# A three-stage attention and FFN kernel: five weight conversions, two attentions, two weight sums and twelve y stores are put elsewhere

## Chip, cores, metric

One core of one Trainium2 chip. The metric is the device time of one execution in microseconds (us); lower is better.

## What is computed

The inputs are `x` (8 batches, 8 heads, 512 positions, 64 wide) and `state` (8, 8, 32, 64), and five weights that arrive as 64-bit floats. Per batch and head, x reads the state and the state reads x:

```python
a = softmax(scale * x @ state.T);   xread = a @ state      # 512 rows
a2 = softmax(scale * state @ x.T);  sread = a2 @ x         # 32 rows
X = concat([xread, sread], axis=2)                          # 544 rows per batch, heads side by side: 512 wide
h = relu(X @ moe_w_in);             Y = (h * h) @ moe_w_out # 512 -> 2048 -> 512
out = (((Y @ w1) * (Y @ w2)) @ w3) @ w_out2                 # 512 -> 1024 -> 1024 -> 512
```

## The kernel before, in words

Matmuls run on pairs of halves: a 32-bit float is written as a high and a low part (`split`, L81 to L83: a cast on ScalarE, a subtraction on VectorE), and a product takes three passes. Since xread is `a @ state`, the kernel forms `state @ w_in` per batch once (`make_sw`, L480) and multiplies it with the turned softmax `aT` (`h_tile`, L515).

**First stage.** A list `order` holds the tiles (c, f): batch c of the 512-row reads, f one of the 16 blocks of 128 of the 2048 inner columns. A tile's hidden block is 6 matmuls and its part of Y 12 more (`y_tile`, L558, two tiles later). 96 tiles are in the list, for batches 0 to 5. Batches 6 and 7, `PAIR`, are left to the second stage. Two tables, `side` and `late`, say which other jobs are written beside tile i: the attention of a later batch (`att_steps`, L304; `att_slots`, L439), the loads of x, and the conversions of 64-bit weights. `issue_after` keeps a job from being ordered ahead of a named instruction; within that, the order on each engine is a scheduler's.

**Conversions.** `load_later` (L218) brings a 128 x 512 block of 64-bit words into a tile named `raw` (four buffers, which the loads `xb` of x share). `convert64` (L139) makes 32-bit floats of it: `low_words` (L124) scales the low words, on ScalarE (L132) or on VectorE (L136), and four VectorE instructions follow (L148, L149, L150, L153). `make_later` (L228) turns the blocks of `w3` once more (L233) and stores the result to memory from a tile `cw` (two buffers: a block of `w3` takes both, one ahead of the turn and one behind it). `load_next` (L668) issues the load of a block three conversions ahead. 40 such blocks are converted beside tiles 32 to 94. The blocks of `w_in` and `moe_w_out` were done before. The set `scalar_keys` (L665) names every second of the later conversions, whose low words go to ScalarE.

**Second stage.** Batches 6 and 7 multiply `moe_w_out` in seven block products in place of eight (`segment`, L892), in four segments q. The weights' sums that this needs, S1 to S4, are formed from `w_scr`, the weight in memory, by `load_s` (L844): one load into `s_in` and accumulating transfers issued by GpSimd on top of it; S2 is S1 plus a block and S4 is S2 plus a block, in the same tile. The segments' results go to `y_scr` in memory, from the second segment on as accumulating transfers (`y_put`, L885).

**Tail and third stage.** Then the 256 state reads of all batches (`h_tile(B, f)`, f from 2 to 15, L1025), with the splits of `w_out2` and the loads of `w3`. Here `add_part` (L212) adds five separately stored parts of Y in memory, 1 MB each. Then `w34_rows` (L1054) forms `w3 @ w_out2`, and `load_w`, `make_w` (L1111, L1120) bring half s of `w1` and `w2`, 512 columns each: the first of the first half's loads is issued at 676.4 us, the last of the second half's at 938.7 us. The rest, from about 740 us, is the second FFN.

GpSimd issues its transfers in program order, each when what it waits for has come. SyncE issues most other transfers, also in order.

## Time and profile before

| | before |
|---|---|
| median of 3 runs | 1245.02 us (1242.31 to 1245.95) |
| the profiled execution's own time | 1242.97 us |
| its span, first to last instruction | 1241.2 us |
| TensorE busy | 1207.4 us (97%) |
| VectorE, ScalarE, GpSimd busy | 923.3, 705.6, 163.2 us |
| mean granted TensorE clock | 0.993 |

The profile is of one execution. A busy time is the sum over an engine's instructions; an idle time stands in brackets before the instruction that ended it, with the instruction or transfer that came last. PE is TensorE, DVE VectorE, ACT ScalarE, POOL GpSimd, SP SyncE. The granted clock is a share of 2.4 GHz.

### The profile page before, as it was taken

Reading aid. Unit: us, or ns where it says so; the run is one execution under the profiler, and the core shown is the slowest. Engines: PE = TensorE matmul, PEld = TensorE weight load, DVE = VectorE, ACT = ScalarE, POOL = GpSimd, SP = SyncE. Lnnn points to the kernel's source line nnn. Section 1 sums busy time; section 2 is a strip of 40 time slices with the busy share of each in tenths; the row PEclk is TensorE's granted clock in tenths of the full one; section 3 lists DMA queues with packets and bytes.
Section 4 is the critical chain, followed back from the end, with each engine's and each line's share of the span. In section 5 each row is a group of like instructions: output and inputs, shape, how many; then the busy total and the mean of one; then the engine's idle time right before and its main releaser. Section 6 shows DMA issues by size and latency. Waiting matters only on the chain.

```text
span 1241.2 us, 18904 instructions
## 1 busy us (share of the span) xinstructions
PE 1207.4 (97%) x7020; PEld 985.4 (79%) x7020; DVE 923.3 (74%) x1648; ACT 705.6 (57%) x1282; POOL 163.2 (13%) x223
## 2 busy tenths in 40 slices
PE   8999999999999989999999899999999999999998
PEld 5677776777767757667788778989898989898988
DVE  7968877678876755566686786787787857877877
ACT  6867556656655645676768554545354635453542
POOL 0000023333320100213241000000000000302110
PEclk9999999999999989999999999999999999999999
DMA  9545768746583532536689954041322450706244
GB/s 259 170 137 190 186 212 230 176 152 147 131 227 100 168 113 94 121 96 87 93 130 244 270 186 154 21 150 42 129 74 96 148 175 18 153 22 149 45 75 136
DMA packets 160916, 170.85 MB, mean 138 GB/s; under 512 B 82232, under 2 KB 114744, under 8 KB 160312
## 3 DMA queue, kind: packets, MB, share of 16 engines
q1 hardware_dynamic: 124296, 110.65, 29.3%
q0 software_dynamic: 36240, 58.73, 23.0%
q8 instruction: 55, 0.90, 0.3%
q14 instruction: 37, 0.30, 0.1%
q10 hardware_dynamic: 288, 0.26, 0.1%
HBM read 107.09 MB, written 67.76 MB: 141 GB/s over the span
## 4 chain that ended last, share of the span: by engine, by line
PE 76%; DMA 8%; DVE 7%; ACT 4%; issue 3%; POOL 1%; SPq 0%; DVEq 0%; POOLq 0%; ACTq 0%
PE y L570 16%; PE qa L1236 11%; PE qd L1236 7%; PE oa L1388 5%; PE od L1388 4%; PE qc L1236 4%; PE qe L1236 4%; DMA s_in<-wscr 3%; DMA raw<-in_moe_w_dram 2%; PE ps_sw L486 2%; PE ab L1298 2%; PE oe L1388 2%; PE oc L1388 2%; PE qa L907 1%; PE ps_w L1061 1%
## 5 line engine op out<-in xcount | busy, mean ns | idle before, releaser
L570 PE MATMUL y<-ghl,wo 128*128 128x512 f32 x1152 | 282.8, 394 | 1.8 <-ACT yo L583 1.4
L570 PEld LDWEIGHTS y<-ghl,wo 128*128 128x128 f32 x1152 | 215.4, 189 | 61.0 <-issue 12.6
L1244 ACT COPY s<-qa 128x512 f32<-128x512 f32 x96 | 56.4, 588 | 181.2 <-PE qa L1236 181.2
L1236 PE MATMUL qa<-yq,wq 128*128 128x512 f32 x576 | 143.9, 389 | 0.0
L83 DVE TENSOR_TENSOR ghl<-r,ghl 128x512 fp32r<-128x512 f32 (+1 forms) x112 | 72.8, 650 | 93.7 <-ACT ghl L82 89.9
L1236 PEld LDWEIGHTS qa<-yq,wq 128*128 128x128 f32 x576 | 107.6, 188 | 22.0
L1236 PE MATMUL qd<-yq,wq 128*128 128x512 f32 x384 | 97.4, 389 | 0.0
L83 DVE TENSOR_TENSOR z<-q,z 128x512 fp32r<-128x512 f32 x112 | 74.2, 686 | 24.4 <-ACT z L82 24.4
L1428 POOL DMA_DIRECT2D out_dram<-o x24 | 28.6, 1604 | 481.6 <-DVE o L1418 481.6
L1236 PEld LDWEIGHTS qd<-yq,wq 128*128 128x128 f32 x384 | 72.1, 188 | 15.0
L82 ACT CAST z<-q 128x512 fp32r<-128x512 f32 x112 | 68.3, 626 | 19.8 <-PE oe L1388 7.4
L1248 DVE TENSOR_TENSOR s<-qa,s 128x512 f32<-128x512 f32 x32 | 22.1, 692 | 69.8 <-ACT s L1244 69.8
L513 ACT ACTIVATE r<-r 128x512 f32<-128x512 f32 (+1 forms) x112 | 67.5, 602 | 2.8
L82 ACT CAST ghl<-r 128x512 fp32r<-128x512 f32 (+1 forms) x112 | 66.1, 590 | 2.7
L83 DVE TENSOR_TENSOR yq<-yraw,yq 128x512 fp32r<-128x512 f32 x98 | 64.3, 683 | 2.3 <-ACT yq L82 2.3
L82 ACT CAST yq<-yraw 128x512 fp32r<-128x512 f32 x98 | 59.5, 625 | 7.8 <-DVE yraw L1165 4.2
L1061 PE MATMUL ps_w<-wo,w3T 128*128 128x512 f32 x192 | 46.4, 401 | 5.9 <-ACT u L82 3.2
L1236 PE MATMUL qc<-yq,wq 128*128 128x512 f32 x192 | 48.7, 389 | 0.0
L1236 PE MATMUL qe<-yq,wq 128*128 128x512 f32 x192 | 48.7, 389 | 0.0
L1061 PEld LDWEIGHTS ps_w<-wo,w3T 128*128 128x128 f32 x192 | 36.8, 194 | 14.9 <-ACT u L82 3.6
L486 PE MATMUL ps_sw<-win,stT 64*32 64x512 f32 (+1 forms) x528 | 39.2, 585 | 6.3 <-ACT r L511 4.8
L1190 DVE TENSOR_TENSOR q<-q,q 128x512 f32<-128x512 f32 x64 | 43.1, 683 | 0.0
(695 smaller groups left out, 2522.0 us busy)
## 6 DMA issues: line engine op xcount, KB each, us to landing
yraw<-yscr SPq DMA_DIRECT2D x56, 256.0 KB, 5.4
yscr<-yo SPq DMA_DIRECT2D x44, 256.0 KB, 2.7
raw<-in_moe_w_out_dram SPq DMA_DIRECT2D x16, 512.0 KB, 4.1
raw<-in_moe_w_dram POOLq DMA_DIRECT2D x64, 128.0 KB, 3.5
raw<-in_moe_w_dram POOLq DMA_DIRECT2D x16, 512.0 KB, 4.6
raw<-in_moe_w_in_dram SPq DMA_DIRECT2D x12, 512.0 KB, 4.4
out_dram<-o SPq DMA_DIRECT2D x24, 256.0 KB, 2.9
out_dram<-o POOLq DMA_DIRECT2D x24, 256.0 KB, 6.2
```

The source lines that it names most:

```text
L82: nc.scalar.copy(hi, src)
L83: return nc.vector.tensor_tensor(out=lo, in0=src, in1=f32(hi), op=ALU.subtract)
L486: mm = nc.tensor.matmul(pss[r][k * NS:(k + 1) * NS, cols], st_of(b)[rows, k, :], win_t[fg][rows, k, cols], start=True, stop=True, tile_pos ...
L513: nc.scalar.activation(r[:, :n], r[:, :n], ACTF.Square)
L570: nc.tensor.matmul(y_ps[c, d][:, :n], wo_t[f][:, wi, d * P:(d + 1) * P], t[:, gi, :n], start=(f == f0 and k == 0), stop=(f == f1 - 1 and k ...
L1061: nc.tensor.matmul(ps, t[:, wi, (j % 4) * P:(j % 4 + 1) * P], wo2_t[j][:, vi, :], start=(j == 0 and k == 0), stop=(j == N1 - 1 and k == 2),)
L1190: return nc.vector.tensor_tensor(out=t, in0=a, in1=b, op=ALU.subtract)
L1236: nc.tensor.matmul(ps, W[w, kt][:, wi, m * P:(m + 1) * P], Y[v, kt][:, vi, :], start=(first and kt == 0 and k == 0), stop=(last and kt == ...
L1244: left["copy"] = nc.scalar.copy(t, ps)
L1298: nc.tensor.matmul(pss[i][:, :NT9], w[:, wi, m * P:(m + 1) * P], Y[B, d][:, vi, :NT9], start=(d == 0 and k == 0), stop=(d == ND - 1 and k ...
L1388: nc.tensor.matmul(ps[tp][:, t % 2 * NH:(t % 2 + 1) * NH], Z[v, idx][:, vi, t * P:(t + 1) * P], rhs[:, wi], start=(first and t % 2 == 0 an ...
L1428: nc.gpsimd.dma_start(dst, src, accum_op=ALU.add)
```

## The change

- **Five conversions behind the pair.** The last five of the 40 blocks are loaded and converted in the tail, beside f = 4, 7, 10, 13 and 15 of the state reads, with one `raw` and one `cw` buffer. The other 35 are spread over the same tiles as the 40 were. The blocks of `w1` and `w2` are ordered by half, so that the five belong to the second half.
- **Low words.** `scalar_keys` is gone: the 20 conversions that it named scale their low words on VectorE, as the others did.
- **Attentions.** The attention of batch 6 starts at tile 72 in place of 74; batches 5 and 6 use the short list of slots that batch 7 had (11 tiles). Batch 6's turned softmax is stored to memory and loaded at tiles 80 and 83, as batch 7's was and is; the turning of batch 7's x comes three tiles later.
- **Two sums in memory.** S2 and S4 of all four segments are formed in memory beside tiles 56, 62, 68, 75 and 82, by one accumulating or plain transfer of 1 MB each, issued by GpSimd. `load_s` then loads S2 and S4 plainly; S1 and S3 are made as before. Three sums are fetched at the stage's start in place of one.
- **Parts of Y.** The five 1 MB `add_part` transfers move from the tail to tiles 88 and 92 and into segments 1, 2 and 3.
- **y stores.** Those of batches 3, 4 and 5 are issued by ScalarE, not SyncE; two of batch 5's four output tiles use the buffers named `r`.

```diff
--- before.py
+++ after.py
@@ -97,6 +97,7 @@
     att_cm = tc.tile_pool(name="att", bufs=1)
     att = att_cm.__enter__()
 
+    room = [att]
     win_t = [None] * NFG
     wo_t = [None] * NF
     raws = {}
@@ -105,7 +106,7 @@
 
         if early:
             return wpool.tile([P, 512, 2], I32, tag="wo", bufs=NF, name=name)
-        return att.tile([P, 512, 2], I32, tag="raw", bufs=4, name=name)
+        return room[0].tile([P, 512, 2], I32, tag="raw", bufs=4 if room[0] is att else 1, name=name)
 
     def load64(key, src, early=False, queue=nc.sync):
 
@@ -140,7 +141,7 @@
 
         t = raws.pop(key)
         if key not in lows:
-            low_words(key, t, key[0] == "win0" or key in early_keys or key in scalar_keys, out if key[0] == "win0" else None)
+            low_words(key, t, key[0] == "win0" or key in early_keys, out if key[0] == "win0" else None)
         hw, r, m = t[:, :, 1], lows.pop(key), out.bitcast(I32)
         if len(out.shape) == 3:
             hw, r = (v.rearrange("p (k n) -> p k n", n=out.shape[2]) for v in (hw, r))
@@ -199,10 +200,10 @@
     later = [(wo2_s[j * P:(j + 1) * P, :], w_out2[j * P:(j + 1) * P, :]) for j in range(N1)]
     w3_v = w3.rearrange("(i d q) (a c) -> i a q d c", d=2, q=NS, a=4)
     later += [(w3_s[:, 2 * i:2 * i + 2], [w3_v[i, a] for a in range(4)]) for i in range(2 * N1)]
-    for src, dst in ((w1, w12_s[0]), (w2, w12_s[1])):
+    for h, src, dst in ((0, w1, w12_s[0]), (0, w2, w12_s[1]), (1, w1, w12_s[0]), (1, w2, w12_s[1])):
         later += [
             (dst[k][:, h, :], src[k * P:(k + 1) * P, h * 512:(h + 1) * 512])
-            for k in range(src.shape[0] // P) for h in range(2)
+            for k in range(src.shape[0] // P)
         ]
 
     stores = []
@@ -226,7 +227,7 @@
             )
 
     def make_later(i):
-        w = att.tile([P, 512], F32, tag="cw", bufs=2, name="cw")
+        w = room[0].tile([P, 512], F32, tag="cw", bufs=2 if room[0] is att else 1, name="cw")
         convert64(("later", i), w)
         if i in turned:
             m, w = w, att.tile([P, 512], F32, tag="cw", bufs=2, name="cw")
@@ -293,7 +294,7 @@
 
     turned_s, turned_a = {}, {}
     aT_t = {}
-    aT_s = {(b, r): dram.tile([P, 2, 512], F32, name=f"aTs{b}_{r}") for b in (2, B - 1) for r in range(G)}
+    aT_s = {(b, r): dram.tile([P, 2, 512], F32, name=f"aTs{b}_{r}") for b in (2, *PAIR) for r in range(G)}
 
     def load_aT(b, r):
         aT_t[b, r] = pa.tile([P, 2, 512], F32R, tag=f"aT{r}", bufs=2, name=f"aT{r}")
@@ -383,7 +384,7 @@
                 ps = bank_m("ps_a") if b else bank_y(2 + r, "ps_a")
                 for j in range(J):
                     turned_a[b] = nc.tensor.transpose(ps[:, j * P:(j + 1) * P], e[:, j * P:(j + 1) * P], ident)
-            if b == B - 1:
+            if b in PAIR:
                 hi, lo = (att.tile([P, 512], F32R, tag="xT", bufs=4, name="aTp") for _ in range(2))
                 last = split(hi, lo, ps)
                 for i, half in enumerate((hi, lo)):
@@ -440,7 +441,7 @@
         if b >= B:
             return [[] for _ in range(NF)]
         xp, sc, s2, s1a, s1b, at, a2t, sr, srt = att_steps(b)
-        if b == B - 1:
+        if b > BLK + 1:
             return [
                 [sc], [], [s2[0], s1a[0]], [s1b[0], s2[1]], [a2t[0]], [at[0], s1a[1]],
                 [a2t[1]], [s1b[1]], [sr], [at[1]], [srt],
@@ -572,7 +573,7 @@
                     start=(f == f0 and k == 0), stop=(f == f1 - 1 and k == 2),
                 )
             if f == f1 - 1:
-                pool, tag = (pa, "yo") if d < 2 or c >= PAIR[0] - 1 else (att, "yo2")
+                pool, tag = (pa, "yo") if d < 2 or c == B else (pa, "r") if c == PAIR[0] - 1 else (att, "yo2")
                 o = pool.tile([P, 512], F32, tag=tag, bufs=2, name="yo")
                 if c == B:
                     nc.scalar.copy(o[:, :n], y_ps[c, d][:, :n])
@@ -581,7 +582,7 @@
                     nc.vector.tensor_copy(o[:, :n], y_ps[c, d][:, :n])
                 else:
                     nc.scalar.copy(o[:, :n], y_ps[c, d][:, :n])
-                nc.sync.dma_start(y_scr[c][part][:, d, :], o[:, :n])
+                (nc.scalar if BLK <= c < B else nc.sync).dma_start(y_scr[c][part][:, d, :], o[:, :n])
 
 
     st = []
@@ -662,11 +663,10 @@
     convs += [("later", i) for i in range(len(later))]
     convs = [("wo", f) for f in range(1, 4)] + convs
     early_keys = [("wo", 0), *convs[:8]]
-    scalar_keys = convs[27::2]
     pos = [0, 0]
 
     def load_next():
-        k = convs[pos[0]] if pos[0] < len(convs) else None
+        k = convs[pos[0]] if pos[0] < len(convs) - behind_pair else None
         pos[0] += 1
         if k:
             {"wo": load_wout, "win": load_win, "later": load_later}[k[0]](*k[1:])
@@ -715,7 +715,8 @@
     side[9] = [sr1]
     side[10] = [srt1]
     ends_at = NF * PAIR[0]
-    spread = [32 + k * (ends_at - 32) // 40 for k in range(40)]
+    behind_pair = 5
+    spread = [32 + k * (ends_at - 32) // (40 - behind_pair) for k in range(40 - behind_pair)]
     for i in [*range(7, 11), *range(15, 31), *spread]:
         side[i].append(conv)
     for i, fgs in ((6, (0, 1)), (10, (1, 1))):
@@ -730,13 +731,15 @@
         side[2 + g].append(lambda g=g: load_xj(2, g))
     for i, steps in enumerate(att_slots(2)):
         late[5 + i] = steps
-    for b, i0 in zip(range(BLK, B), (32, 48, 60, 74, 85)):
+    for b, i0 in zip(range(BLK, B), (32, 48, 60, 72, 85)):
         for i, steps in enumerate(att_slots(b)):
             late.setdefault(i0 + i, []).extend(steps)
         for g in range(G):
             side[i0 - 8 + g].append(lambda b=b, g=g: load_xb(b, g))
-            side[i0 - 6 + g].append(lambda b=b, g=g: turn_x(b, g))
-            side[i0 - 2 + g + (b == B - 1)].append(lambda b=b, g=g: load_xn(b, g))
+            side[i0 - (6 if b < B - 1 else 3) + g].append(lambda b=b, g=g: turn_x(b, g))
+            side[i0 - 2 + g].append(lambda b=b, g=g: load_xn(b, g))
+    for g in range(G):
+        side[80 + 3 * g].append(lambda g=g: load_aT(PAIR[0], g))
 
     c0, c1 = PAIR
     MH = DM // 2
@@ -755,6 +758,13 @@
         for half in (HI, LO):
             side[32 + 2 * f + half].append(lambda f=f, half=half: paced(save_wo, f, half))
     side[40].append(lambda: nc.sync.dma_start(st_s, stT[:, PAIR[0]:]))
+    for i in (88, 92):
+        side[i].append(lambda: paced(add_part))
+    A_w = {f"{i}{j}": w_scr[:, :, j - 1, (i - 1) * MH:i * MH] for i in (1, 2) for j in (1, 2)}
+    s_mem = {n: dram.tile([P, NF // 2, MH], F32, name=f"smem{n}") for n in (2, 4)}
+    for i, n, src in ((56, 2, A_w["21"]), (62, 2, A_w["22"]), (68, 2, A_w["11"]), (75, 4, s_mem[2]), (82, 4, A_w["12"])):
+        op = {} if i in (56, 75) else {"accum_op": ALU.add}
+        side[i].append(lambda n=n, src=src, op=op: paced(lambda: nc.gpsimd.dma_start(s_mem[n], src, **op)))
 
     for _ in range(3):
         load_next()
@@ -838,18 +848,20 @@
 
     s_steps = []
     for q in range(NFG):
-        wq = {f"{i}{j}": w_scr[:, 2 * q:2 * q + 2, j - 1, (i - 1) * MH:i * MH] for i in (1, 2) for j in (1, 2)}
-        s_steps += [(q, 1, wq["21"], wq["22"]), (q, 2, None, wq["11"]), (q, 4, None, wq["12"]), (q, 3, wq["11"], wq["21"])]
-    s_in = []
+        us = slice(2 * q, 2 * q + 2)
+        s_steps += [
+            (q, 1, A_w["21"][:, us], A_w["22"][:, us]), (q, 2, s_mem[2][:, us], None),
+            (q, 4, s_mem[4][:, us], None), (q, 3, A_w["11"][:, us], A_w["21"][:, us]),
+        ]
 
     def load_s():
         if s_steps:
             q, n, first, more = s_steps.pop(0)
-            if first is not None:
-                s_in[:] = [yp.tile([P, 2, MH], F32, tag="sr", bufs=3, name="s_in")]
-                nc.sync.dma_start(s_in[0], first)
-            nc.gpsimd.dma_start(s_in[0], more, accum_op=ALU.add)
-            s_next.append((q, n, s_in[0]))
+            t = yp.tile([P, 2, MH], F32, tag="sr", bufs=3, name="s_in")
+            nc.sync.dma_start(t, first)
+            if more is not None:
+                stores.append(nc.gpsimd.dma_start(t, more, accum_op=ALU.add))
+            s_next.append((q, n, t))
 
     s_next = []
 
@@ -969,6 +981,8 @@
 
         def fill(i):
             if i == 0:
+                if q:
+                    paced(add_part)
                 make_sw(c0, n, banks=lambda r, name: bank_h(name))
             elif i == 1:
                 role_h(n, "B11", 0)
@@ -991,7 +1005,8 @@
 
         return fill
 
-    load_s()
+    for _ in range(3):
+        load_s()
     role_h(0, "B11", 0)
     role_h(0, "B11", 1)
     prep(0, "B11")
@@ -1009,7 +1024,9 @@
     role_h(0, "B22", 1)
     for q in range(NFG):
         def tail(i):
-            if i == 4:
+            if i == 0:
+                paced(add_part)
+            elif i == 4:
                 split_x9(0)
                 split_x9(1)
             elif i > 4:
@@ -1020,16 +1037,20 @@
     yp_cm.__exit__(None, None, None)
     w34_cm = tc.tile_pool(name="w34p", bufs=1, reuse_waits="tile")
     w34p = w34_cm.__enter__()
+    room[0] = w34p
+    rest_keys = list(range(len(later) - behind_pair, len(later)))
     for j in range(N1 // 2):
         load_wo2(j)
     for f in range(2, NF):
         h_tile(B, f)
+        if f in (4, 7, 10, 13, 15):
+            make_later(rest_keys.pop(0))
+        if f in (2, 4, 7, 10, 13):
+            load_later(rest_keys[0])
         if f < N1 + 2:
             split_wo2(f - 2)
         if f in (4, 6, 8, 10):
             load_w3(N1 // 2 + f // 2 - 2)
-        if f % 3 == 0:
-            paced(add_part)
         pend.append((B, f))
         while len(pend) > 2:
             y_tile(*pend.pop(0))
```

**Place 1: ScalarE, batch 5, tiles f = 3 to 5, before.** `r` and `ghl` are a tile's hidden block and its halves, `raw` is a 64-bit block whose conversion comes later.

```order
L511 ACTIVATE r<-ph_3__4523 128x512
L513 ACTIVATE r<-r 128x512
L132 ACTIVATE raw<-raw 128x512
L82 CAST ghl<-r 128x512
L511 ACTIVATE r<-ph_4__4592 128x512
L513 ACTIVATE r<-r 128x512
L82 CAST ghl<-r 128x512
L132 ACTIVATE raw<-raw 128x512
L511 ACTIVATE r<-ph_5__4632 128x512
L513 ACTIVATE r<-r 128x512
L82 CAST ghl<-r 128x512
```

The same place now:

```order
L512 ACTIVATE r<-ph_3__4542 128x512
L514 ACTIVATE r<-r 128x512
L82 CAST ghl<-r 128x512
L512 ACTIVATE r<-ph_4__4584 128x512
L514 ACTIVATE r<-r 128x512
L82 CAST ghl<-r 128x512
L512 ACTIVATE r<-ph_5__4611 128x512
L514 ACTIVATE r<-r 128x512
L82 CAST ghl<-r 128x512
```

The two instructions on `raw` between the tiles' instructions are gone from ScalarE; nothing takes their place.

**Place 2: GpSimd, the conversions of `w3`, before** (`raw` is a load of a 64-bit block in four pieces, `w3s` the store of a converted one).

```order
L224 DMA raw<-in_moe_w_dram 32x2x512 x3
L235 DMA w3s<-cw 128x512 x3
L224 DMA raw<-in_moe_w_dram 32x2x512 x12
L235 DMA w3s<-cw 128x512
L224 DMA raw<-in_moe_w_dram 32x2x512 x4
L235 DMA w3s<-cw 128x512
```

The same place now, beside tiles 54 to 64 (`smem_321` is the sum S2 in memory):

```order
L236 DMA w3s<-cw 128x512
L767 DMA smem_321<-wscr 1024x256
L225 DMA raw<-in_moe_w_dram 32x2x512 x4
L236 DMA w3s<-cw 128x512
L225 DMA raw<-in_moe_w_dram 32x2x512 x4
L236 DMA w3s<-cw 128x512
L225 DMA raw<-in_moe_w_dram 32x2x512 x4
L236 DMA w3s<-cw 128x512
L767 DMA smem_321<-wscr 1024x256
L225 DMA raw<-in_moe_w_dram 32x2x512 x4
```

The queue held loads and stores alone; two of the 1 MB sums now stand in it, each behind a store and ahead of a load.

**Place 3: VectorE in the tail, f = 4 to 6, before** (`w` is a split of `w_in`, `wo` one of `w_out2`).

```order
L508 TENSOR_TENSOR r<-ph_4__6389,r 128x256
L83 TENSOR_TENSOR w_6519<-win_1293,w_6519 128x512
L83 TENSOR_TENSOR ghl<-r,ghl 128x256
L508 TENSOR_TENSOR r<-ph_5__6422,r 128x256
L83 TENSOR_TENSOR w_6552<-win_1293,w_6552 128x512
L83 TENSOR_TENSOR ghl<-r,ghl 128x256
L83 TENSOR_TENSOR wo_6342<-wst_6302,wo_6342 128x512
L83 TENSOR_TENSOR wo_6377<-wst_6302,wo_6377 128x512
L508 TENSOR_TENSOR r<-ph_6__6453,r 128x256
L83 TENSOR_TENSOR w_6584<-win_1293,w_6584 128x512
L83 TENSOR_TENSOR ghl<-r,ghl 128x256
```

The same place now:

```order
L509 TENSOR_TENSOR r<-ph_4__6377,r 128x256
L137 TENSOR_SCALAR raw<-raw 128x512
L149 TENSOR_SCALAR cw<-raw 128x512
L83 TENSOR_TENSOR w_6524<-win_1297,w_6524 128x512
L150 TENSOR_SCALAR cw<-cw 128x512
L83 TENSOR_TENSOR ghl<-r,ghl 128x256
L151 SCALAR_TENSOR_TENSOR cw<-raw,cw 128x512
L509 TENSOR_TENSOR r<-ph_5__6419,r 128x256
L154 ISA cw<-raw,cw 128x1024
L83 TENSOR_TENSOR w_6557<-win_1297,w_6557 128x512
L83 TENSOR_TENSOR ghl<-r,ghl 128x256
L83 TENSOR_TENSOR wo_6331<-wst_6289,wo_6331 128x512
```

A conversion's five instructions (L137, L149, L150, L151, L154, the old L136 to L153) now stand between the state reads' splits.

## Rows read from the trace of the kernel before

**Rows 1.** Stretches: length, then PE, PEld, DVE, ACT, POOL busy (xcount), PEclk, DMA, GB/s.

```profile
150.00:480.00 330.00, 318.89 (x1861) 243.61 (x1860) 245.46 (x488) 195.88 (x350) 79.79 (x141) 0.98 0.60 161
480.00:645.00 165.00, 158.32 (x833) 119.38 (x832) 101.90 (x128) 107.94 (x167) 39.83 (x42) 1.00 0.56 104
645.00:700.00 55.00, 55.00 (x297) 47.14 (x296) 35.02 (x66) 40.85 (x95) 9.51 (x6) 1.00 1.25 249
700.00:724.00 24.00, 18.06 (x71) 13.96 (x70) 22.21 (x46) 15.49 (x32) 0.00 (x0) 0.93 0.73 261
```

**Rows 2.** Timeline of PE, its waits: start, length, line, shape, [idle before, releaser].

```profile
193.09 3.35 PE L570 MATMUL y<-ghl,wo 128*128 128x512 f32 x12 [1.40 <-ACT yo L583]
218.96 1.09 PE L486 MATMUL ps_sw<-win,stT 64*32 64x512 f32 x14 [2.51 <-ACT r L511]
370.18 1.09 PE L486 MATMUL ps_sw<-win,stT 64*32 64x512 f32 x14 [2.29 <-ACT r L511]
445.24 1.96 PE L327 MATMUL ps_s<-xT,stT 64*32 64x512 f32 x14 [4.53 <-DVE x9T L426]
...
545.90 1.67 PE L830 MATMUL ph1B__5513<-aT,sw 128*128 128x512 f32 x6 [1.48 <-ACT gB L835]
580.77 1.65 PE L830 MATMUL ph2B__5786<-aT,sw 128*128 128x512 f32 x6 [0.86 <-ACT gB L835]
...
704.11 11.13 PE L1061 MATMUL ps_w<-wo,w3T 128*128 128x512 f32 x48 [3.19 <-ACT u L82]
718.45 18.01 PE L1061 MATMUL ps_w<-wo,w3T 128*128 128x512 f32 x71 [2.45 <-DVE w3T L83]
```

**Rows 3.** Timeline of ACT, low words ahead of three of PE's waits.

```profile
217.25 0.65 ACT L132 ACTIVATE raw<-raw 128x512 int32<-128x512 uint32 x1 [4.79 <-DMA raw<-in_moe_w_dram]
368.99 0.65 ACT L132 ACTIVATE raw<-raw 128x512 int32<-128x512 uint32 x1 [4.04 <-DMA raw<-in_moe_w_dram]
441.81 0.65 ACT L132 ACTIVATE raw<-raw 128x512 int32<-128x512 uint32 x1 [7.03 <-DMA raw<-in_moe_w_dram]
```

**Rows 4.** Busy time in three stretches behind PE's waits; columns as in rows 1.

```profile
370.00:375.00 5.00, 4.82 (x24) 3.15 (x25) 3.09 (x5) 3.40 (x8) 0.40 (x1) 0.66 0.87 284
445.00:451.00 6.00, 5.76 (x25) 3.35 (x26) 5.19 (x11) 1.96 (x4) 1.08 (x2) 0.57 0.25 79
718.00:724.00 6.00, 5.55 (x17) 4.43 (x18) 5.47 (x13) 2.74 (x6) 0.00 (x0) 0.72 0.89 294
```

**Rows 5.** Timeline of ACT, its waits for transfers in the second stage and the tail.

```profile
542.84 0.62 ACT L82 CAST s_hl<-s_in 128x512 fp32r<-128x512 f32 x1 [3.45 <-DMA s_in<-wscr]
...
685.72 0.62 ACT L82 CAST wq<-wraw 128x512 fp32r<-128x512 f32 x1 [3.22 <-DMA wraw<-w12s]
691.16 1.67 ACT L82 CAST wq<-wraw 128x512 fp32r<-128x512 f32 x3 [4.30 <-DMA wraw<-w12s]
```

**Rows 6.** Timeline of DVE, one conversion, from L136 to L153.

```profile
445.10 0.42 DVE L136 TENSOR_SCALAR raw<-raw 128x512 int32<-128x512 uint32 x1
...
447.07 0.69 DVE L153 CUSTOM_DVE_ANT_0 cw<-raw,cw 128x1024 uint16<-128x1024 uint16 x1
```

**Rows 7.** DMA issues: engine, count, KB each, median us from issue to landing.

```profile
raw<-in_moe_w_dram POOLq DMA_DIRECT2D x64, 128.0 KB, 3.5
raw<-in_moe_w_dram POOLq DMA_DIRECT2D x16, 512.0 KB, 4.6
yscr<-yscr POOLq DMA_DIRECT2D x5, 1024.0 KB, 18.7
w3s<-cw POOLq DMA_DIRECT2D x16, 256.0 KB, 2.6
```

**Rows 8.** Tile `yscr`, its transfers, the additions among them, us to landing.

```profile
DMA to landing us min/median/max: 1.8/4.7/27.8
```

**Rows 9.** Chain of waits, ahead of PE's wait at 218.96: start us, us, what.

```profile
212.10 5.05 DMA raw<-in_moe_w_dram
```

**Rows 10.** Tile opart: ACT's two DMA issues, ns min/median/max.

```profile
L1476 ACTq DMA_DIRECT2D out_dram<-opart x2: 338/358/377, 1237.3 to 1238.0; - x2
```

## The prediction

> **What bounds the kernel now.** The sum is made against the profiled execution, 1242.97 us; the median of three runs is 2.05 us above it (0.16%). The busy time by stretch comes first: TensorE (PE) is busy through all 55 us of the first part of the tail, but misses 330 − 318.89 = 11.11 us in the first stage from 150 us on, 165 − 158.32 = 6.68 in the second stage and 24 − 18.06 = 5.94 at the tail's end [rows 1]. No product is added or taken away, so the change can win only these 23.7 us and the clock lost behind them. PE's timeline tells what the gaps waited for: in the first stage four waits make 1.40 + 2.51 + 2.29 + 4.53 = 10.73 us; in the second, two waits for ScalarE's (ACT's) `gB` make 1.48 + 0.86 = 2.34; at the tail's end two make 3.19 + 2.45 = 5.64 [rows 2].
>
> ACT's timeline shows what is behind three of the first four. Just ahead of each, ACT has reached a low-word instruction (L132) and stands idle there, 4.79, 4.04 and 7.03 us, for a 64-bit block that is still being loaded [rows 3]. ACT works in order, and the tile's own activation and split stand behind it (place 1). PE's waits, 2.51, 2.29 and 4.53 us, are some 2.2 us shorter than ACT's: so much cover the engines have ahead of PE. The fourth, 1.40 us at 193.09, is for `yo`, the end of a batch.
>
> Two waits of the first stage and one of the tail cost more than their length. In the 5 us from 370 on the granted clock is 0.66, in the 6 us from 445 on 0.57, and from 718 on 0.72, with PE busy nearly throughout [rows 4]; each is a mean of stretches at 1.2 and at 2.4 GHz, after PE had stood still. The work lost is (1 − 0.66) × 5 = 1.70, (1 − 0.57) × 6 = 2.58 and (1 − 0.72) × 6 = 1.68 us.
>
> **The change, part by part.**
>
> A. *Low words to DVE, first stage.* ACT loses 20 instructions of 0.65 us [rows 3], and with them its waits for loads. VectorE (DVE) takes 20 × 0.42 = 8.4 us [rows 6] and gives five whole conversions away, of 447.07 + 0.69 − 445.10 = 2.66 us each [rows 6], 13.3 in all: of its 245.46 us [rows 1] it is relieved of 4.9. On DVE a low word stands directly ahead of its own conversion, whose load was issued three conversions earlier. 35 conversions over some 320 us are 9.1 us apart, so a load has 27 us, where its median is 3.5 [rows 7]. Hence nothing waits there: −2.51 − 2.29 − 4.53 − 1.70 − 2.58 = −13.6. What is late next are the ends of batches, three of which now have their y stores issued by ACT, and the attention of batch 6, two tiles earlier. For these I add 1 us; the bounds are −1.4 (the wait for `yo` goes too) and +4.2 (three more like it).
>
> B. *Second stage.* At 542.84 ACT stood idle 3.45 us for a sum `s_in` that was still being accumulated [rows 5], and 3 us later PE waited for ACT's `gB`. S2 and S4 become plain loads, and three sums are fetched early in place of one. I take the two waits for `gB` as gone, −2.34; the bounds are 0 (ACT is late by its own work) and −6.68, all the idle time of the stage.
>
> C. *Tail.* Before its end ACT stands 3.22 and 4.30 us for `wraw`, converted weights on their way from memory [rows 5]; the DMA engines' share is the highest of the four stretches, 1.25 [rows 1], with five 1 MB additions, 18.7 us each, among their work [rows 7]. DVE then is busy 22.21 of 24 us [rows 1], and PE waits. Without the additions `wraw` should come sooner, and 5.94 + 1.68 = 7.62 us could go. But five conversions put 13.3 us of work into the 55 − 35.02 = 20 us that DVE has free ahead (place 3), and part of that idle time only spaces the tiles. The last block is loaded into the one `raw` buffer when the conversion before it is done, 4.6 us [rows 7], with some 3.6 us of other DVE instructions between the two; and the splits that PE waits for stand behind it. I take −2; the bounds are −7.6 and +3.7 (a wait of 2 us for that load, and 1.7 of clock).
>
> D. *Seven 1 MB transfers into the first stage, three into the second.* I count 0: a raw load has 27 us of lead, the median addition takes 18.7 [rows 7], and the DMA shares are 0.60 and 0.56 [rows 1]. If this cover is gone, it is the slow rival below.
>
> E. *Twelve y stores on ACT; batch 6's `aT` stored and reloaded.* A DMA issue by ACT takes 0.36 us [rows 10], twelve 4.3, of an engine that is idle 330 − 195.88 = 134 us [rows 1]: 0, but for ACT's wait for copies by DVE, which the 1 us of A holds. The reload of `aT` is far ahead of its use in the second stage: 0.
>
> Sum: −13.6 + 1 − 2.34 − 2 = −16.9, that is 1226.0 us against the profiled execution; with half of the 2.05 us to the median, **1227.0**. The least that the parts allow is 1242.97 − 13.6 − 1.4 − 6.68 − 7.6 = 1213.7.
>
> **The rivals.**
>
> *The waits move to DVE.* If loads come late, DVE stands at the low word as ACT did, and the tile's split stands behind it. Then A brings nothing: 1242.97 − 2.34 − 2 + 1 = 1239.6. For it speak ACT's waits of up to 7.03 us for blocks [rows 3]. Against it: those low words stood well ahead of their conversions, at the moment when the block was landing; of the conversions themselves no row shows DVE waiting for a load.
>
> *The tail is bound by DVE.* C is +3.7 in place of −2: 1226.0 + 5.7 + 1 = 1232.7. For it: DVE is full in the last 24 us. Against: ACT's two waits there, 7.5 us, held DVE up as well, and they should shrink.
>
> *Slower: stores wait behind the sums on GpSimd's queue.* A block of `w3` takes both `cw` buffers, so its second one must wait until the last block's store has landed, 2.6 us [rows 7] in the trace. Beside these blocks three sums (tiles 56, 62, 68) are issued, each behind a store (place 2). If a sum of S us holds the queue, the next store, issued 9.1 us later, lands S + 2.6 us after the sum's issue, and the conversion that needs its buffer comes at 18.2. With S = 18.7 DVE stands 3.1 us; with 27.8, the longest landing of `yscr` [rows 8], 12.2 us. Less the cover of 2.2 us, and with 1.70 or 2.58 of clock, a sum costs 2.6 or 12.6 us, three of them 7.8 or 37.8: 1234.8, or **1264.8** on the side of this rival. It eats the gain of 16.9 (5.6 each) from a wait of DVE of some 5.8 us, that is from S = 21.4. For it: an addition did take 27.8. Against: those additions came five close together into the busiest stretch, and in pieces of 128 elements, where the sums have 256 (place 2). A raw load issued behind an accumulating transfer of 256 KB landed in 5.05 us in the chain of waits [rows 9], against the median of 3.5: a transfer ahead in the queue delays by little there.
> The Trainium skill bears on this (DMA: Bandwidth & Descriptors, section "Two DMAs through the same engine are not ordered"): descriptors within one queue of a DMA engine start in order. By that rule a store issued behind a sum starts behind it and this rival's 1264.8 follows if the sum is long enough; the trace agrees with the order, by the 5.05 us, and has no transfer of 1 MB with a store behind it.
>
> *It does not do what it says.* The loads were late near 370 and 441 us because the DMA engines were busy, and the next reader of memory (`aT`, `xb`) takes the place of `raw`; the second stage and the tail give nothing: 1243 to 1246.
>
> **How the numbers follow.** The forecast within its bounds (1214 to 1231) has 0.54, the tail bound by DVE 0.13, the waits on DVE 0.14, the slow rival 0.12, no effect 0.07. About 0.3%, 3.7 us, is what a measurement of this kernel can tell from no change, so faster means under 1241.3. The first two and most of the third are that: 0.79. No effect and the rest of the third: 0.09. The slow rival: 0.12. The range holds the forecast and the two rivals on its side with 1 us of room: 1215 to 1241; the slow rival and no effect lie outside, 0.19.
>
> **What would show it.** A: no idle time of ACT for `raw`, PE idle in the first stage under 4 us, clock 1.00 behind. B: no wait of ACT for `s_in` over 2 us, and PE idle under 5 us in the second stage. C: shorter waits of ACT for `wraw`; PE idle at the tail's end 3 to 5 us. If DVE waits there for `raw`, the second rival holds. D: sums that land in under 20 us, and no wait of DVE for a `w3s` store; if there is one beside the sums, the slow rival holds. The prediction is wrong if PE's idle time in the first stage stays over 8 us, or if PE's busy time itself grows.

## The result, and the profile after

The changed kernel takes 1225.38 us (median of 4 runs, 1224.48 to 1228.12), the kernel before beside it 1244.67; the ratio is 0.9851, with a 95% interval of 0.9828 to 0.9873. It is faster by 1.5%, within the range and 1.6 us under the 1227.0 that was forecast. Its profiled execution took 1224.62 us (span 1222.8, mean clock 0.997).

Busy time by stretch, columns as in [rows 1]. The second stage starts 18 us earlier than before, the tail 24 and the products of the third stage 16 to 18, so the bounds of the stretches are moved; the last two rows are pieces of the tail:

```profile
150.00:470.00 320.00, 320.00 (x1956) 248.70 (x1955) 244.86 (x485) 188.37 (x335) 83.60 (x138) 1.00 0.74 185
470.00:630.00 160.00, 157.71 (x790) 121.22 (x789) 104.29 (x132) 112.76 (x180) 37.28 (x36) 1.00 0.73 136
630.00:700.00 70.00, 62.50 (x295) 51.26 (x293) 55.37 (x114) 43.83 (x99) 4.83 (x9) 0.95 0.63 207
700.00:724.00 24.00, 23.03 (x116) 19.40 (x117) 20.57 (x46) 13.90 (x32) 0.00 (x0) 1.00 0.55 195
635.00:640.00 5.00, 5.00 (x24) 4.30 (x23) 3.56 (x8) 4.51 (x11) 0.92 (x2) 0.73 0.67 206
655.00:660.00 5.00, 5.00 (x21) 4.28 (x21) 3.56 (x9) 4.04 (x11) 1.07 (x2) 0.68 0.63 200
```

TensorE (PE) has no idle time in the first stage, where 11.11 us were [rows 1], 2.29 in the second stage, where 6.68 were, and 7.50 + 0.97 = 8.47 in the tail, where 5.94 were. The half clock that followed two waits of the first stage [rows 4] now follows two waits of the tail, and costs (1 − 0.73) × 5 + (1 − 0.68) × 5 = 2.95 us.

The waits, from PE's timeline (columns as in [rows 2]):

```profile
493.42 1.67 PE L840 MATMUL ph0B__5257<-aT,sw 128*128 128x512 f32 x6 [0.55 <-ACT gB L845]
...
633.06 0.50 PE L543 MATMUL y<-ghl,wo 128*128 128x512 f32 x1 [2.06 <-DVE ghl L83]
653.57 0.50 PE L543 MATMUL y<-ghl,wo 128*128 128x512 f32 x1 [1.84 <-DVE ghl L83]
680.34 4.84 PE L1082 MATMUL ps_w<-wo,w3T 128*128 128x512 f32 x20 [1.32 <-ACT e L1094]
687.22 11.16 PE L1082 MATMUL ps_w<-wo,w3T 128*128 128x512 f32 x48 [1.13 <-ACT u L82]
...
700.97 5.55 PE L1082 MATMUL ps_w<-wo,w3T 128*128 128x512 f32 x23 [1.84 <-DVE w3T L83]
```

The waits for `gB` of the second stage shrank to 0.55 us in all; the tail has waits of a new kind, for `ghl`, ahead of its old ones. VectorE's (DVE's) timeline tells why: each of the five conversions there begins with a wait for its block.

```profile
630.97 0.43 DVE L137 TENSOR_SCALAR raw<-raw 128x512 int32<-128x512 uint32 x1 [4.66 <-DMA raw<-in_moe_w_dram]
...
640.15 0.43 DVE L137 TENSOR_SCALAR raw<-raw 128x512 int32<-128x512 uint32 x1 [0.54 <-DMA raw<-in_moe_w_dram]
...
650.62 0.43 DVE L137 TENSOR_SCALAR raw<-raw 128x512 int32<-128x512 uint32 x1 [2.29 <-DMA raw<-in_moe_w_dram]
...
661.39 0.43 DVE L137 TENSOR_SCALAR raw<-raw 128x512 int32<-128x512 uint32 x1 [0.73 <-DMA raw<-in_moe_w_dram]
...
675.44 0.43 DVE L137 TENSOR_SCALAR raw<-raw 128x512 int32<-128x512 uint32 x1 [6.07 <-DMA raw<-in_moe_w_dram]
```

4.66 + 0.54 + 2.29 + 0.73 + 6.07 = 14.3 us. The first stands just ahead of PE's wait at 633.06, the third ahead of the one at 653.57, and the fifth among the splits of `w3T` and `wq` ahead of the last three.

The transfers, from the view of DMA issues (columns as in [rows 7]):

```profile
raw<-in_moe_w_dram POOLq DMA_DIRECT2D x16, 512.0 KB, 7.0
...
yscr<-yscr POOLq DMA_DIRECT2D x5, 1024.0 KB, 13.7
...
smem<-wscr POOLq DMA_DIRECT2D x4, 1024.0 KB, 10.1
```

A sum in memory lands in 10.1 us (the median of four, the first of them a plain copy of 8.3), not in the 18.7 that the additions took in the tail before [rows 7]; the additions themselves take 13.7 at their new places.

### The profile page after: what moved, and what is told of

Its sections match the earlier page's. It is cut to its first block, busy times and chain, and to the rows that moved or that the text cites. A ratio compares the mean times of both kernels' runs of the same rounds, so it can differ in the third digit from the quotient of the medians.

```text
span 1222.8 us, 18863 instructions
## 1 busy us (share of the span) xinstructions
PE 1201.5 (98%) x7020; PEld 985.5 (81%) x7020; DVE 930.8 (76%) x1668; ACT 694.4 (57%) x1262; POOL 160.1 (13%) x220
## 4 chain that ended last, share of the span: by engine, by line
PE 86%; DVE 5%; issue 3%; ACT 3%; DMA 2%; POOL 0%; DVEq 0%; SPq 0%; ACTq 0%; POOLq 0%
PE y L571 21%; PE qa L1257 11%; PE qd L1257 7%; PE oa L1409 5%; PE od L1409 4%; PE qc L1257 4%; PE qe L1257 4%; PE ps_sw L487 2%; PE qa L919 2%; PE ab L1319 2%; PE oe L1409 2%; PE oc L1409 2%; PE ps_w L1082 1%; DMA raw<-in_moe_w_dram 1%; PE qd L919 1%
## 5 line engine op out<-in xcount | busy, mean ns | idle before, releaser
L571 PE MATMUL y<-ghl,wo 128*128 128x512 f32 x1152 | 280.0, 392 | 0.0
L1082 PEld LDWEIGHTS ps_w<-wo,w3T 128*128 128x128 f32 x192 | 35.6, 188 | 13.6 <-ACT u L82 2.2
L1257 PEld LDWEIGHTS qe<-yq,wq 128*128 128x128 f32 x192 | 36.0, 188 | 7.5
```

Of the source, the lines that this page charges most:

```text
L571: nc.tensor.matmul(y_ps[c, d][:, :n], wo_t[f][:, wi, d * P:(d + 1) * P], t[:, gi, :n], start=(f == f0 and k == 0), stop=(f == f1 - 1 and k ...
L1082: nc.tensor.matmul(ps, t[:, wi, (j % 4) * P:(j % 4 + 1) * P], wo2_t[j][:, vi, :], start=(j == 0 and k == 0), stop=(j == N1 - 1 and k == 2),)
L1257: nc.tensor.matmul(ps, W[w, kt][:, wi, m * P:(m + 1) * P], Y[v, kt][:, vi, :], start=(first and kt == 0 and k == 0), stop=(last and kt == ...
```

## Experiments

All times are medians of runs beside the kernel before on the same chip, where that kernel took 1244.18 to 1245.11 us, and the ratio is to it.

| kernel | us | ratio (95%) |
|---|---|---|
| before, low words on VectorE | 1225.16 | 0.985 (0.9829 to 0.987) |
| changed | 1225.38 | 0.9851 (0.9828 to 0.9873) |
| changed, low words back on ScalarE | 1243.72 | 0.9999 (0.9986 to 1.0013) |
| changed, sums as before | 1235.17 | 0.9933 (0.9915 to 0.995) |
| changed, additions back in the tail | 1243.43 | 0.9993 (0.9983 to 1.0003) |
| changed, tail without four loads | 1217.38 | 0.9788 (0.977 to 0.9805) |
| changed, two raw buffers in the tail | 1217.67 | 0.9782 (0.9761 to 0.9802) |
| changed, no conversions in the tail | 1223.94 | 0.9838 (0.9819 to 0.9857) |
| the same, stores on SyncE | 1227.91 | 0.987 (0.9854 to 0.9885) |
| the same, half sums | 1214.43 | 0.9764 (0.9747 to 0.978) |
| the same, sums as before | 1219.83 | 0.9796 (0.9777 to 0.9815) |
| changed, y stores on SyncE | 1224.26 | 0.9837 (0.9817 to 0.9857) |
| changed, batch 6 not parked | 1227.07 | 0.9858 (0.9838 to 0.9879) |

### The low words, alone and undone

The kernel before, with one line changed:

```diff
-    scalar_keys = convs[27::2]
+    scalar_keys = []
```

> The kernel before, with one edit: the 20 low words that stood on ScalarE go to VectorE. Theory (the waits of the first stage come from ScalarE standing at a block that is still landing): ScalarE's idle time for raw goes, PE's idle time from 150 to 480 us falls from 11.1 us to under 2, the clock behind it is 1.00, and the time falls by 9.3 us of waits and 4.3 of clock, to about 1231 us. First rival (the waits move to VectorE): PE stays idle for 8 us or more there, 1240 us or above. Second rival (the 35 blocks at wider spacing, the y stores on ScalarE or the attentions' new places made the gain, not the low words): under half of it, 1238 us or above.

Measured: 1225.16 us, as fast as the whole change. By busy time the first stage has no idle time any more. What follows comes some 17 us earlier; by stretches moved with it, the second stage and the tail are nearly as they were, 162 − 155.30 = 6.70 us idle (6.68 before) and 77 − 71.73 = 5.27 (5.94 before):

```profile
150.00:480.00 330.00, 330.00 (x2023) 255.43 (x2022) 257.63 (x518) 193.30 (x343) 81.18 (x142) 1.00 0.62 168
468.00:630.00 162.00, 155.30 (x778) 116.87 (x767) 101.16 (x127) 106.72 (x166) 40.15 (x41) 0.99 0.57 104
630.00:707.00 77.00, 71.73 (x363) 59.98 (x362) 55.70 (x109) 54.73 (x124) 8.96 (x5) 1.00 1.10 250
```

From 150 to 470 us, engines stood 28.3 us in nine waits for 64-bit blocks before; here 0.4 us in one.

The opposite edit puts the set back into the changed kernel:

```diff
-            low_words(key, t, key[0] == "win0" or key in early_keys, out if key[0] == "win0" else None)
+            low_words(key, t, key[0] == "win0" or key in early_keys or key in scalar_keys, out if key[0] == "win0" else None)
...
+    scalar_keys = convs[27::2]
```

> The changed kernel, with the low words of every second later conversion back on ScalarE. Theory: the waits come back where loads land, PE is idle again for 6 us or more in the first stage, with 2 to 4 us of clock behind; 1233 to 1240 us. Rival (the wider spacing and the other moves are enough): PE idle under 2 us there, within 3 us of 1225.

Measured: 1243.72 us, no different from before and 3.7 above the range of the theory. ScalarE's timeline shows two of its waits at a low word, PE's the wait behind each:

```profile
419.18 0.65 ACT L133 ACTIVATE raw<-raw 128x512 int32<-128x512 uint32 x1 [13.01 <-issue]
...
444.45 0.68 ACT L133 ACTIVATE raw<-raw 128x512 int32<-128x512 uint32 x1 [4.41 <-DMA raw<-in_moe_w_dram]
```

```profile
420.36 2.42 PE L526 MATMUL ph__4505<-aT,sw 128*128 128x512 f32 x6 [3.87 <-ACT r L512]
...
451.30 1.63 PE L487 MATMUL ps_sw<-win,stT 64*32 64x512 f32 x14 [1.97 <-ACT r L512]
```

For the longer wait the profile names no transfer, but its block's load, issued at 408.84, took 10.3 us to land, until 419.1; it stood 3.54 us behind a 1 MB sum on GpSimd's queue. So the 18 us that the low words cost here need not be the same as the 19 in the kernel before: a part of them may come with the sums.

Both rivals fall: the waits did not move to DVE, which is busy 257.63 of 330 us with the low words on it, and the wider spacing does not help ScalarE. It also says that the rest of the change is worth nothing in sum, which the next runs take apart. Not tried: low words that stay on ScalarE but stand later, at their conversion. The edit moves them to another engine and to another place at once.

### The tail

Without four of the five loads, so that DVE has the same work and no block to wait for but the first:

```diff
         if f in (4, 7, 10, 13, 15):
+            t = raws["later", rest_keys[0]]
             make_later(rest_keys.pop(0))
-        if f in (2, 4, 7, 10, 13):
+            if rest_keys:
+                raws["later", rest_keys[0]] = t
+        if f == 2:
             load_later(rest_keys[0])
```

> The changed kernel with four of the five loads in the tail left out, so that all five conversions there run on the first block. VectorE's work is the same; its waits for loads are gone but for the first. Theory (the tail loses by the late blocks, for which VectorE stands 14.3 us, and not by the work): VectorE's idle time for raw falls to under 5 us, PE's idle time in the tail from 8.5 to 3 to 5 us, 1218 to 1222 us. Rival (13.3 us of work is too much for VectorE there): PE idle 7 us or more in the tail, 1224 us or above.

Measured: 1217.38 us. PE is idle for 70 − 65.76 = 4.24 us in the tail, and DVE waits for one block, 4.97 us:

```profile
630.00:700.00 70.00, 65.76 (x319) 54.62 (x318) 62.94 (x130) 48.85 (x110) 2.93 (x5) 0.98 0.63 209
```

So the four late blocks cost some 8 us. The work itself, with DVE busy 62.94 of 70 us, costs less: of the 4.24 us, one wait of 2.38 us at 633.22 stands behind that first block, and with no conversion in the tail 0.22 us are left (below). The same can be had with all loads made, one conversion ahead:

```diff
-        return room[0].tile([P, 512, 2], I32, tag="raw", bufs=4 if room[0] is att else 1, name=name)
+        return room[0].tile([P, 512, 2], I32, tag="raw", bufs=4 if room[0] is att else 2, name=name)
...
-        t = w34p.tile([P, 2, 512], F32, tag="wst2", bufs=4, name="wst2")
+        t = w34p.tile([P, 2, 512], F32, tag="wst2", bufs=3, name="wst2")
...
+        if f == 2:
+            load_later(rest_keys[0])
+            load_later(rest_keys[1])
         if f in (4, 7, 10, 13, 15):
             make_later(rest_keys.pop(0))
-        if f in (2, 4, 7, 10, 13):
-            load_later(rest_keys[0])
+            if len(rest_keys) > 1:
+                load_later(rest_keys[1])
```

> The changed kernel with two buffers for raw in the tail, blocks loaded one conversion ahead (three stage buffers for wst in place of four make the room). Theory (late blocks are what the tail loses by): VectorE's idle time for raw falls from 14.3 us to under 7, PE's idle time in the tail from 8.5 to 3 to 5 us; 1217 to 1221 us. Rival (with three stage buffers the loads of w3 come late and PE waits for w3T): PE idle over 6 us in the tail, 1223 us or above.

Measured: 1217.67 us; DVE waits 2.7 us for blocks, and PE has two waits in the tail, of 2.40 and 1.22 us. The fourth stage buffer was not missed. The busy time:

```profile
630.00:700.00 70.00, 66.31 (x322) 55.34 (x322) 61.61 (x127) 50.16 (x111) 4.30 (x8) 0.98 0.69 229
```

The additions, back where they were:

```diff
-    for i in (88, 92):
-        side[i].append(lambda: paced(add_part))
...
-                if q:
-                    paced(add_part)
...
-            if i == 0:
-                paced(add_part)
-            elif i == 4:
+            if i == 4:
...
+        if f % 3 == 0:
+            paced(add_part)
```

> The changed kernel with the five 1 MB additions of Y's parts back in the tail. Theory (they slow the loads of raw and wraw there): the blocks' loads take 8 us or more, VectorE stands over 20 us for them, PE's idle time in the tail grows from 8.5 to 12 us or more, 1229 to 1236 us. Rival (nothing waits for them, the DMA engines have room): within 2 us of 1225.

Measured: 1243.43 us, 18 above the changed kernel and above the theory's range. DVE stood 29.6 us for blocks; PE's timeline has a single wait that is longer than any in the kernel before:

```profile
639.82 0.79 PE L543 MATMUL y<-ghl,wo 128*128 128x512 f32 x1 [9.14 <-DVE ghl L83]
...
676.19 0.79 PE L543 MATMUL y<-ghl,wo 128*128 128x512 f32 x1 [4.00 <-DVE ghl L83]
```

The stretch from 630 to 700 us has a clock of 0.88 there, 8.4 us of full-speed work:

```profile
630.00:700.00 70.00, 52.11 (x241) 42.50 (x241) 38.29 (x79) 32.12 (x76) 12.44 (x13) 0.88 0.91 210
```

The five conversions and the five additions cannot share the tail. Taking the additions out is also a gain by itself: with the additions there and no conversions (the first run above) PE idles 5.27 us in the tail, with neither (the run with the sums as before and no conversions in the tail, below) 0.23; the two take 1225.16 and 1219.83 us.

All 40 conversions beside the first stage:

```diff
-    behind_pair = 5
+    behind_pair = 0
...
-        if f in (4, 7, 10, 13, 15):
+        if rest_keys and f in (4, 7, 10, 13, 15):
             make_later(rest_keys.pop(0))
-        if f in (2, 4, 7, 10, 13):
+        if rest_keys and f in (2, 4, 7, 10, 13):
```

> The changed kernel with all 40 conversions beside the first stage, none in the tail. Theory (the five conversions cost the tail what the moved additions gave it: VectorE stands 14.3 us at blocks that are landing, PE waits 2.06 and 1.84 us of it and loses 1.65 of clock): PE's idle time in the tail falls from 8.5 us to 3 to 5, the first stage stays without a wait since VectorE is busy only 249 of 330 us there; 1218 to 1221 us. Rival (40 blocks in the first stage are too many with the sums in memory beside them): waits of 4 us or more come back in the first stage, 1225 us or above.

Measured: 1223.94 us, between the two. The tail is clean, as the theory had it, better even: 0.22 us idle. And there is one new wait in the first stage, as the rival had it (PE's timeline):

```profile
370.74 3.51 PE L487 MATMUL ps_sw<-win,stT 64*32 64x512 f32 x30 [7.08 <-DVE x9T L427]
```

The chain of waits ahead of it (start us, us, what), and DVE's timeline:

```profile
353.99 1.38 POOL smem L767
355.37 0.58 POOL raw L120
355.95 1.03 issue
...
356.99 13.04 DMA w12s<-cw
```

```profile
370.06 0.43 DVE L149 TENSOR_SCALAR cw<-raw 128x512 f32<-128x512 f32 x1 [5.62 <-DMA w12s<-cw]
```

A store of a converted block, issued by GpSimd 3.00 us behind a 1 MB sum, with a 512 KB load between the two, takes 13.04 us to land, where the median of the 16 such stores in that run is 5.0; the conversion that needs its `cw` buffer waits, and PE with it. This is the slow rival of the prediction, at one place: the sum took 14.1 us, the rival's S + 2.6 makes 16.7 from the sum's issue, and the store landed after 3.00 + 13.04 = 16.04. Where no sum is issued (the run with the sums as before, below), the store at this place (354.64) landed in 6.1 us. With 35 conversions at 9.1 us PE does not wait, with 40 at 8.0 it does.

### The queue behind the sums

On top of the run without conversions in the tail, the stores are issued by SyncE:

```diff
-        store = nc.gpsimd.dma_start(later[i][0], w)
+        store = nc.sync.dma_start(later[i][0], w)
```

> All 40 conversions beside the first stage, as in the run without conversions in the tail, and the stores of the converted blocks issued by SyncE in place of GpSimd. There, VectorE stood 5.62 us for a store of w12 that GpSimd had issued 3 us behind a sum of 1 MB and that took 13.04 us to land; PE waited 7.08 us. Theory (the store started only when the sum ahead of it in GpSimd's queue was through): from SyncE it lands in under 6 us, the 7.08 us and the clock behind them go, 1212 to 1217 us. Rival (the DMA engines were full then, and a store is late from any queue): PE still waits 4 us or more near 370 us, 1221 us or above; or SyncE's own loads, queued behind the stores' waits, come late and PE waits for x or aT elsewhere.

Measured: 1227.91 us, no faster than with the stores on GpSimd. The wait of 7.08 us is gone, but PE idles 320 − 313.87 = 6.13 us in the first stage and 160 − 155.99 = 4.01 in the second. Three of its waits:

```profile
225.02 0.66 PE L406 MATMUL ps_a<-ident,e 128*128 128x128 f32 x4 [1.90 <-DVE sw L83]
226.81 2.91 PE L526 MATMUL ph__2437<-aT,sw 128*128 128x512 f32 x6 [1.13 <-DVE sw L83]
...
509.35 2.25 PE L840 MATMUL ph0B__5302<-aT,sw 128*128 128x512 f32 x6 [2.48 <-ACT gB L845]
```

The run does not test the theory, because the edit moved the sums too. They are ordered behind the last store (`paced`), and that store no longer stands in GpSimd's queue. GpSimd issues the five between 178.46 and 217.76 us, where they stood between 286.84 and 412.34 in the run before it. The last two (GpSimd's timeline):

```profile
211.75 0.52 POOL L767 DMA_DIRECT2D smem<-smem  x1 [10.94 <-DMA smem<-wscr]
217.76 1.34 POOL L767 DMA_DIRECT2D smem<-wscr  x1 [4.36 <-DMA smem<-smem]
```

No sum stands beside the stores of `w12` any more, which begin at 372.78. Their median landing is 2.2 us, the longest 8.8, and no wait of DVE for a store is over 3.17 us; whether the other queue or the missing sums did that stays open. Ahead of the first two waits of PE, DVE had stood 4.59 us, until 219.24, for a block whose load GpSimd issued at 212.26, just behind a sum. Ahead of the last one, ACT had stood 3.25 us, until 507.26, for a `y` store.

The Trainium skill (DMA: Bandwidth & Descriptors, section "Two DMAs through the same engine are not ordered") states that within one queue of a DMA engine descriptors start in order and are pipelined. The landing at 16.04 us in the run before this one fits that order. It does not prove it: from 355 to 370 us the DMA share is 1.00 to 1.23 there, so the DMA engines were busy as well, which was the rival.

Each sum in two halves, three tiles apart, all still on GpSimd's queue:

```diff
-        side[i].append(lambda n=n, src=src, op=op: paced(lambda: nc.gpsimd.dma_start(s_mem[n], src, **op)))
+        for h in range(2):
+            k8 = slice(h * NF // 4, (h + 1) * NF // 4)
+            side[i + 3 * h].append(lambda n=n, src=src, op=op, k8=k8: paced(
+                lambda: nc.gpsimd.dma_start(s_mem[n][:, k8], src[:, k8], **op)))
```

> All 40 conversions beside the first stage, none in the tail, and each of the five sums issued as two transfers of 512 KB three tiles apart, still by GpSimd. Theory (a store behind a sum waits for the sum's length): half sums land in about 7 us, no store of a converted block takes over 9, and PE's wait of 7.08 us goes; 1212 to 1218 us. Rival (it is not the length of one transfer but the number of bytes beside the conversions): waits of 4 us in all remain, 1221 us or above.

Measured: 1214.43 us, the fastest of all, 2.4% under the kernel before; the mean clock of its profile is 1.000. PE's waits in the first stage are 0.28 us, in the tail 0.22:

```profile
150.00:470.00 320.00, 319.72 (x1949) 246.99 (x1948) 253.92 (x510) 187.02 (x333) 95.31 (x153) 1.00 0.78 197
470.00:630.00 160.00, 156.90 (x783) 120.37 (x782) 105.08 (x133) 112.72 (x179) 36.03 (x35) 1.00 0.72 133
630.00:700.00 70.00, 69.78 (x350) 58.69 (x349) 56.37 (x110) 53.40 (x117) 0.00 (x0) 1.00 0.64 205
```

The bytes are the same, so it is not their number alone. But the halves did not land in 7 us:

```profile
smem<-wscr POOLq DMA_DIRECT2D x8, 512.0 KB, 9.2
```

That median mixes plain and accumulating halves: the first sum's two, plain, took 4.1 and 6.2 us, the accumulating ones 7.5 to 10.8. The longest store still took 10.2 us, against the theory's 9, and DVE still waits up to 2.81 us for stores beside the sums, too little to reach PE. Whether the shorter transfer or its other place did it is not settled by this run.

### Sums, y stores, parking

The changed kernel with S2 and S4 formed on the chip, as before:

```diff
-    for i, n, src in ((56, 2, A_w["21"]), (62, 2, A_w["22"]), (68, 2, A_w["11"]), (75, 4, s_mem[2]), (82, 4, A_w["12"])):
-        op = {} if i in (56, 75) else {"accum_op": ALU.add}
-        side[i].append(lambda n=n, src=src, op=op: paced(lambda: nc.gpsimd.dma_start(s_mem[n], src, **op)))
...
-            (q, 1, A_w["21"][:, us], A_w["22"][:, us]), (q, 2, s_mem[2][:, us], None),
-            (q, 4, s_mem[4][:, us], None), (q, 3, A_w["11"][:, us], A_w["21"][:, us]),
...
+        s_steps += [(q, 1, wq["21"], wq["22"]), (q, 2, None, wq["11"]), (q, 4, None, wq["12"]), (q, 3, wq["11"], wq["21"])]
...
-    for _ in range(3):
-        load_s()
+    load_s()
```

> The changed kernel with S2 and S4 formed on the chip as before, by accumulating transfers, and no 1 MB transfers for them in the first stage. Theory (the plain loads took PE's waits for gB away): ScalarE waits again 3 us for s_in, PE's idle time in the second stage goes from 2.4 back to 5 to 8 us; 1228 to 1232 us. Rival (the waits went with something else, or the 1 MB transfers cost the first stage as much): within 2 us of 1225.

Measured: 1235.17 us, above the theory's range (the profile is of an execution of 1239.29 us). ScalarE waits 3.66 us for `s_in` at 493.98, 4.15 at 528.52, and PE for `gB` behind them; the clock falls after it (PE's timeline, then busy time):

```profile
496.10 2.92 PE L836 MATMUL ph0B__5243<-aT,sw 128*128 128x512 f32 x6 [3.24 <-ACT gB L841]
```

```profile
490.00:500.00 10.00, 6.76 (x22) 5.17 (x21) 3.14 (x3) 4.87 (x7) 1.19 (x1) 0.76 0.45 80
```

The same edit and `behind_pair = 0` together give its price without the tail's waits:

> S2 and S4 formed on the chip as before and all 40 conversions beside the first stage; the additions' new places, the attentions' and the y stores' stay. Beside the run with half sums (1214 us) it has no 1 MB sums in the first stage, beside the run of the changed kernel with the sums as before (1235 us) no conversions in the tail. Theory (the sums in memory save waits for gB and the half clock behind them, some 10 us, and the conversions in the tail cost some 8): PE idle in the second stage 6 to 8 us with 3 to 5 us of clock, the tail clean, no wait in the first stage; 1222 to 1227 us. Rival (the sums in memory are worth nothing once the tail is clean): 1213 to 1217 us.

Measured: 1219.83 us, 5.4 above the run with half sums and better than forecast: PE idles 6.33 us in the second stage, the clock there is 0.99, and the tail is clean:

```profile
470.00:630.00 160.00, 153.67 (x750) 116.01 (x749) 101.60 (x127) 107.38 (x169) 43.84 (x42) 0.99 0.72 125
630.00:700.00 70.00, 69.77 (x358) 59.11 (x358) 55.84 (x108) 54.51 (x122) 0.00 (x0) 1.00 0.65 201
```

So the sums in memory are worth some 5 us here (4 by the ratios, whose intervals just touch), and 9.8 beside the conversions in the tail. The tails do not make that difference: PE idles 8.67 us there in the run before and 8.47 in the changed kernel. The second stage does, with 7.57 us of idle time at a clock of 0.97; why it is worse there was not followed.

The last two parts:

```diff
-                (nc.scalar if BLK <= c < B else nc.sync).dma_start(y_scr[c][part][:, d, :], o[:, :n])
+                nc.sync.dma_start(y_scr[c][part][:, d, :], o[:, :n])
```

> The changed kernel with the y stores of batches 3 to 5 on SyncE again. Theory (they lie beside other work on either engine): within 2 us of 1225, no new PE wait at the ends of batches. Rival (SyncE's loads come late behind them): a PE wait of 1 us or more at a batch's end or for x, 1228 us or above.

```diff
-            if b in PAIR:
+            if b == B - 1:
...
-    for g in range(G):
-        side[80 + 3 * g].append(lambda g=g: load_aT(PAIR[0], g))
```

> The changed kernel with batch 6's turned softmax kept on the chip, not stored to memory and loaded again. Theory (the store and the reload are hidden, DMA share 0.73 beside them): within 2 us of 1225. Rival (the two transfers of 512 KB take room from blocks and sums): 2 to 4 us faster, with shorter waits of VectorE for stores.

Measured: 1224.26 and 1227.07 us, both within 2 us of the changed kernel, and their intervals overlap with its own. Neither moves a wait of the first stage. Both theories hold: the y stores on ScalarE and the parking, which is the way of batch 6's turned softmax through memory, are worth nothing that can be measured.

## Why the prediction was right, point by point

| term | forecast | measured in the two traces |
|---|---|---|
| A, first stage | −13.6 + 1 | −11.11 − 4.28 = −15.4 |
| B, second stage | −2.34 | 2.29 − 6.68 = −4.4 |
| C, tail | −2 | 8.47 + 2.95 − 7.62 = +3.8 |
| sum | −16.9 | −16.0 |

The spans differ by 18.4 us, so some 2.4 us lie in no row named here.

**A** was right in its mechanism, and it is shown from both sides: the low words alone make the whole gain, and put back, there beside the sums, they take it all. It was sized too small by 2.8 us: I kept the 1.40 us wait for `yo` and added 1 us for ends of batches. Neither is there.

**B** was right: the plain loads took the waits away (ScalarE's longest for `s_in` is 0.28 us), and the run without them brings them back. The size was short by 2 us. I counted two waits for `gB`, 2.34 of the 6.68 us of idle time; the one of 1.59 for `sw` shrank to 0.59 too, and the two shorter ones for `gB`, 1.45 together, to one of 0.55.

**C** is the step that failed. "I take −2; the bounds are −7.6 and +3.7" ended at +3.8, at the bad bound. Its first half came true: with the additions gone, ScalarE's waits for `wraw` fell from 3.22 and 4.30 us to 0.86, and PE's at the tail's end from 5.94 to 4.57. What it had wrong was the loads. It saw the late load of the last block and took 4.6 us for it; that one took 9.2 (issued at 666.12, used at 675.4), and all five were late: four because one buffer forbids loading ahead, the first because it was issued at 622.65 and took 8.3 us. They brought the two waits for `ghl`, 3.90 us, and the 2.95 of clock. By the prediction's own sign (DVE waits there for `raw`) this is its second rival, at its price of +3.7. But that rival's name, "bound by DVE", does not fit: with the same work and four loads fewer the kernel is 8 us faster.

**D** held in the changed kernel, but its price was wrong. The additions of the busiest stretch (18.7 us) were taken for the sums; they land in 10.1. The slow rival came in a neighbour of the change, when the conversions stood 8.0 us apart: the store behind a sum took 13.04 us. Its rule for the landing, S + 2.6, fits with S = 14.1, and its threshold of 21.4 us was far too high there: it let the conversion that needs the buffer come 18.2 us behind the sum's issue, and it stood ready after 370.06 − 5.62 − 353.99 = 10.45. That the store waits for the sum, and not for full DMA engines, stays argued.

**E** held: the y stores and the parking measure nothing.

The total came out within 2 us because A and B were short by 4.9 us and C was off by 5.8 the other way. That is luck.

## What to carry to other kernels

An instruction that waits for a load holds up what stands behind it on its engine, so look at what that is: twenty instructions of 0.65 us on ScalarE cost 19 us that way, and on VectorE, at their own conversions, nothing that can be measured. Moving work into an engine's idle time needs buffers to load ahead as much as it needs the time; here one more buffer was worth 7.7 us. When several parts change together, try each alone: one line made all of the gain. The others made about nothing in sum, because two gains of some 5 us each (the additions out of the tail, the sums in memory) stood against a loss of some 11 (1225.38 against 1214.43, five conversions in the tail, 8 of it by late blocks). And see where an edit moves other work: a store on another queue moved five sums by over 100 us.

## What was not expected of the hardware

A wait of PE can cost more than its length: 4.28 us of lost clock stand beside 11.11 of idle time in the first stage before, 2.95 beside 8.47 in the tail after, 8.4 beside 17.9 from 630 to 700 us with the additions back. It need not: with the y stores on SyncE the same stretch has 10.02 us of idle time, two waits of 2.02 and 2.03 us for `ghl` among it, and a clock of 1.00:

```profile
630.00:700.00 70.00, 59.98 (x289) 48.10 (x289) 55.57 (x115) 43.88 (x99) 4.83 (x9) 1.00 0.62 205
```

In the kernel before, the wait of 2.51 us at 218.96 has full clock behind it too.

The landing of an accumulating transfer of 1 MB is no constant of its size: 18.7 us (12.9 to 27.8) for the five additions of the kernel before, 14.1 for the same five back in the tail beside the conversions, 13.7 at their new places, and 9.2, 11.1 and 11.2 for the three accumulating sums of the changed kernel, which have rows of 256 elements in place of 128. Accumulating halves of sums took 7.5 to 10.8, so half the bytes are not half the time. What sets it was not tried.
